# Windowed attention and two feed-forward nets on one core: the attention's loads in another order, and two pairs of small VectorE operations made one each

## The chip, the cores and the metric

The kernel runs on one core of a Trainium2 chip. The metric is the device time of one execution in microseconds (us), the median over repeated executions. Lower is better.

## What is computed

The reference, cut to what matters:

```python
# batch 4, 8 heads, 512 local and 32 global positions, head size 64, all float32
k_all, v_all = concat([k_g, k_l]), concat([v_g, v_l])
out_g = sm(scale * q_g @ k_all.T) @ v_all                 # global rows see everything
s_ll  = where(abs(i - j) <= 32, scale * q_l @ k_l.T, -1e9)   # local rows see a window
out_l = sm(concat([scale * q_l @ k_g.T, s_ll])) @ v_all   # ... and all global rows
# sm(s): e = exp(s - max(s)); e / (sum(e) + 1e-9)
x = concat([out_g, out_l]) as 2176 rows of 512
h = x @ w_in;  x = (h * cos(h)) @ w_out                   # net 1, 512 -> 2048 -> 512
out = relu(x @ w2_in) ** 2 @ w2_out                       # net 2, same sizes
```

The weights of the nets come as 64-bit numbers, of which the kernel takes the float32 value by operations on their two halves.

## The kernel before

The attention is cut into 40 items. Per batch and per group of four heads there are four local items (a pair of heads, half of the 512 positions each) and then one global item (the 32 global rows of the four heads). A group of four heads is called g0, g1, ... g7 here. Each engine executes its instructions in the order in which they stand in the program, so the program's order is a hand-made pipeline: the loop at line 1365 runs over steps, and in step s each stage treats item s minus the stage's lag. `CFG['order']` says in which order the stages stand within a step, `CFG['lag']` gives the lags. The stages are TRK and KEV and KC (transpose keys on TensorE, copy them out on ScalarE, double them on GpSimd), TRQ and QE (queries), S (scores, TensorE), SM (maximum and exponential), RC (reciprocal of the sum), NM (normalization, GpSimd and one VectorE operation), TM (transposes of the probabilities), TE (their way out of PSUM, ScalarE), OM (product with the values), OE (result to `xt`, VectorE). `BG`, `CB` and `CC` hold background work of the first net that is spread over the steps: loading raw weights and converting them, splitting operands into two halves.

Loads are issued on SyncE's queue (SP), which also works in program order. For each group there are loads of keys (`kn`, LK, five transfers), queries (`qn`, LQ, four transfers), values (`va`, LV, six transfers) and a copy of the values in SBUF, shifted by 64 rows (`vb`, CV, two transfers). `va`, `vb`, `kn` and `qn` have two buffers, so g2 overwrites g0. The two values tiles are `va_93` and `va_94`, their shifted copies `vb_95` and `vb_96`. The global values, padded (`vgz`, four transfers), global queries (`qgn`), key tails (`ktn`) and the raw weights of the first net (`raw`, one transfer of 512 KB each, two buffers) go through the same queue. Transfers take turns on eight semaphores, so a transfer is issued only when the one eight places before it has landed.

The prologue (lines 618 to 639) loads g0 and g1 except for g1's values; these are loaded at the end of step 2 (line 1424) and copied at the end of step 5 (line 1426). From g2 on the stages LK, LQ, LV and CV have lags 0, 1, 8 and 11, counted from the first item of the group two before.

A raw tile is read by three engines: ScalarE (line 147) and GpSimd (line 142) take its two halves, VectorE (lines 151 and 156) goes on with what they made. These stand in the engines' order at fixed steps: the first raw tile's in step 8, the second's ScalarE operation in step 11.

In a global item the scores lie in two PSUM banks. VectorE takes a maximum of each (line 541), then the maximum of both (line 546) and its product with -1/8 (line 547); ScalarE forms the exponentials and two sums (line 551); VectorE adds the sums (line 565), adds 1e-9 (line 568) and takes the reciprocal (line 571). All of these are one element per partition.

After the attention's last items the nets begin. Their order of work is planned by a list scheduler in the kernel itself, which is not touched.

Of the kernel before, what the change touches and what calls it, by code (L numbers as in the profile page):

```python
# [16 lines left out]
ALU = mybir.AluOpType  # L17
# [6 lines left out]
TWOPI = 2.0 * math.pi  # L24


CFG = {'order': ['CV', 'LQ', 'S', 'TE', 'BG', 'LK', 'OM', 'TRK', 'KEV', 'CC', 'SM',
           'RC', 'NM', 'CB', 'LV', 'OE', 'TRQ', 'QE', 'KC', 'TM'],
 'lag': {'S': 0,
         'TRK': -3,  # L30
         'TRQ': -2,
# [7 lines left out]
         'TE': 3,  # L39
         'OM': 4,  # L40
         'OE': 4,
         'LK': 0,
         'LQ': 1,
         'LV': 8,
         'CV': 11},
 'ndv': 1,
# [6 lines left out]
def kernel(  # L53
# [14 lines left out]
    nc = tc.nc  # L68
# [151 lines left out]
    BT, BG, BS, BO = (0, 1), (2,), (3, 4, 5), (6, 7)  # L220
# [20 lines left out]
    def whole(dst, src, c0, queues):  # L241

        n = dst.shape[2]
        if n == 2:
            for h, queue in enumerate(queues):
                queue.dma_start(dst[:, c0:4, h], src[h].rearrange("(c p) d -> p c d", p=P))
        else:
            for c in range(c0, 4):
                r = P * (c - c0)
                queues[0].dma_start(dst[:, c], src[:, r : r + P].rearrange("h p d -> p h d"))  # L250
# [10 lines left out]
    def load_q(gi, h=0, n=4, queues=(nc.sync, nc.sync)):  # L261
        b, g = gi // 2, slice(4 * (gi % 2) + h, 4 * (gi % 2) + h + n)
        if gi not in qn:
            qn[gi] = fp.tile([P, 4, 4, D], F32, tag="qn", name="qn", bufs=2)
        whole(qn[gi][:, :, h : h + n], q_l[b, g], 0, queues)

    def load_v(gi):
        b, h0 = gi // 2, 4 * (gi % 2)
        va, g = VA[gi % 2], slice(h0, h0 + 4)
        nc.sync.dma_start(va[0:SG, 0], v_g[b, g].rearrange("h p d -> p h d"))  # L270
        for c in range(5):
            r0, r1 = (SG if c == 0 else 0), (SG if c == 4 else P)
            nc.sync.dma_start(
                va[r0:r1, c],
                v_l[b, g, P * c - SG + r0 : P * c - SG + r1].rearrange("h p d -> p h d"),
            )
# [29 lines left out]
    def k_evac(p):  # L306
# [4 lines left out]
        if p == 0:  # L311
# [6 lines left out]
            )  # L318
        if CFG["kb"] == "A":
            nc.scalar.activation(  # L320
                t[:, :, 128:KTB], tk[:, 0:SG].unsqueeze(1).to_broadcast([P, 8, SG]), AF.Copy
            )
        elif CFG["kb"] == "D":
            nc.vector.tensor_copy(
# [3 lines left out]
    def k_copy(p):  # L328
# [4 lines left out]
        nc.gpsimd.tensor_scalar(t[:, 0:7, 64:128], t[:, 1:8, 0:64], **one)  # L333
        if CFG["kb"] == "P":
            nc.gpsimd.tensor_scalar(
# [52 lines left out]
    class Local:  # L388
# [48 lines left out]
        def recip(self):  # L437
            st = self.st
            return [
                lambda: nc.vector.tensor_scalar(  # L440
                    st[:, 2, :], st[:, 1, :], 1e-9, None, op0=ALU.add
                ),
                lambda: nc.vector.reciprocal(st[:, 2, :], st[:, 2, :]),
            ]

        def norm(self):
# [7 lines left out]
            for u in range(4):  # L454
                (nc.vector if u < CFG["ndv"] else nc.gpsimd).tensor_scalar(
                    self.pt[:, u, 0:P],
# [14 lines left out]
        def t_evac(self):  # L471
            self.tws = lp.tile([P, 4, P], F32, tag="tws", name="tws", bufs=2)
            self.tgs = lp.tile([P, P], F32, tag="tgs", name="tgs", bufs=2)
            nc.scalar.activation(self.tws, self.tw, AF.Copy)
            if CFG["teg"][self.hb] == "D":
                nc.vector.tensor_copy(self.tgs, self.tg)
# [28 lines left out]
        def o_evac(self):  # L505
            c0 = self.b * SL + 256 * self.hb
            dst, src = xt[:, self.kk, c0 : c0 + 256], self.o.rearrange("p i q -> p (i q)")
            if CFG["oe"][self.hb] == "D":
                nc.vector.tensor_copy(dst, src)
# [4 lines left out]
    class Global:  # L514
# [19 lines left out]
        def softmax(self):  # L534
            self.pt = lp.tile([P, 544], F32, tag="ptg", name="ptg", bufs=1)
            self.st = lp.tile([P, 8], F32, tag="stg", name="stg", bufs=2)
            st = self.st
            n = (320, 224)

            def top(i):  # L540
                nc.vector.tensor_reduce(
                    st[:, i : i + 1], self.s[i][:, 0 : n[i]], op=ALU.max, axis=AX.X
                )

            def rest():
                nc.vector.tensor_tensor(st[:, 2:3], st[:, 0:1], st[:, 1:2], op=ALU.max)
                nc.vector.tensor_scalar(
                    st[:, 2:3], st[:, 2:3], -0.125, None, op0=ALU.mult
                )
                for i in range(2):  # L550
                    nc.scalar.activation(
                        self.pt[:, 320 * i : 320 * i + n[i]],
                        self.s[i][:, 0 : n[i]],
                        AF.Exp,
                        bias=st[:, 2:3],
                        scale=0.125,
                        accum_out=st[:, 4 + i : 5 + i],
                    )

            return [lambda: top(0), lambda: top(1), rest]  # L560

        def recip(self):
            st = self.st
            return [
                lambda: nc.vector.tensor_tensor(
                    st[:, 6:7], st[:, 4:5], st[:, 5:6], op=ALU.add
                ),
                lambda: nc.vector.tensor_scalar(
                    st[:, 6:7], st[:, 6:7], 1e-9, None, op0=ALU.add
                ),  # L570
                lambda: nc.vector.reciprocal(st[:, 6:7], st[:, 6:7]),
            ]
# [64 lines left out]
    copy_v(0)  # L637
    load_k(1, 2, 2)
    load_q(1, 2, 2)
    nc.vector.memset(qgbd, 0.0)  # L640
    nc.gpsimd.memset(masks[0], 0.0)
    for h in range(2):
        s = slice(64 * h, 64 * h + 64)
# [16 lines left out]
    def spin(n):  # L660

        t = ps.tile([P, 512], F32, tag=f"bank{BO[1]}", name="spin")[:, 0:P]
        for _ in range(n):
            nc.tensor.matmul(t, lhsT=idle, rhs=idle, start=True, stop=True)
# [377 lines left out]
    S = [Step(s) for s in range(NS)]  # L1042
# [128 lines left out]
    order = [(s, i) for s in range(NS) for i in range(7)]  # L1171
# [193 lines left out]
    for s in range(L["TRK"], NI + L["OE"]):  # L1365
        due = lambda k: due_tr.get(s - k)
        qe = []
        for c in CFG["order"]:
            if c in ("BG", "CB", "CC"):
                for fn in bg[c].get(s, []):  # L1370
                    fn()
            elif c in ("TRK", "TRQ", "KEV", "KC", "QE"):
                p = due(L[c])
                if p is None:
                    continue
                if c == "TRK":
                    if p == 0:
                        spin(6)
                    tr_k(p)
                    if p == 0:  # L1380
                        spin(2)
                elif c == "TRQ":
                    qe = tr_q(p)
                    if p == 0:
                        spin(2)
                elif c == "KEV":
                    k_evac(p)
                elif c == "KC":
                    k_copy(p)
                elif c == "QE":  # L1390
                    for op in qe:
                        op()
            elif c in ("LK", "LQ", "LV", "CV"):
                p = due(L[c])
                if p is not None and p % 2 == 0 and p // 2 + 2 < 2 * B:
                    dict(LK=load_k, LQ=load_q, LV=load_v, CV=copy_v)[c](p // 2 + 2)
            else:
                i = it(s - L[c])
                if not i:
                    continue  # L1400
                if c == "S":
                    i.s_mm()
                    if s == 0:
                        prep_ktail(0)
                        k_tail(0)
                        k_tail(1)
                    elif s % 10 == 6 and s < 30:
                        prep_ktail(s // 10 + 1)
                    elif s % 10 == 3:
                        prep_qg(s // 10)  # L1410
                elif c == "SM":
                    for op in i.softmax():
                        op()
                elif c == "RC":
                    for op in i.recip():
                        op()
                else:
                    dict(NM=i.norm, TM=i.t_mm, TE=i.t_evac, OM=i.o_mm, OE=i.o_evac)[c]()
        if s in (8, 18):
            load_ktn(s // 10 + 2)  # L1420
        if s in (7, 17, 27):
            load_qgn(s // 10 + 1)
        if s == 2:
            load_v(1)
        if s == 5:
            copy_v(1)
        if due(0) is not None and due(0) // NPAIR + 1 < B:
            if due(0) % NPAIR == 2:
                load_vg(due(0) // NPAIR + 1)
        if s == XBOPEN:  # L1430
            first.close()
            open_pool("xb")
        if s == NI - 1:
            early.close()
            open_pool("s")
        if s >= NI - 1:
            emit(1.55 * (s - NI + 2))
# [39 lines left out]
```

## Time and profile before

| | |
|---|---|
| time, median of 3 runs | 874.62 us (874.11 to 876.35) |
| the profiled execution's own time | 874.08 us |
| its span, first to last instruction | 872.3 us |
| granted TensorE clock, mean | 0.997 of 2.4 GHz |
| TensorE (PE) busy | 849.8 us, 97% |
| VectorE (DVE) busy | 655.6 us, 75% |
| ScalarE (ACT) busy | 530.7 us, 61% |
| GpSimd (POOL) busy | 582.1 us, 67% |
| SP's queue (q1) | 130,736 packets, 179.79 MB, 62.5% of 16 DMA engines |

The span is what the profiler saw of one execution; the execution's time is 1.8 us longer. An engine's busy time leaves out waiting, issuing and branches. A timeline row gives start, length, engine, line, operation, output and inputs and, in brackets, the idle time of the engine just before it with what ended it. A row of the chain gives a piece of the sequence of work that ended last.

### The profile page before, as it was taken

What the parts mean: (1) busy time and instruction counts of PE and PEld (TensorE: products, weight loads), DVE (VectorE), ACT (ScalarE), POOL (GpSimd) and SP (SyncE); (2) the same over time, 40 slices, a digit from 0 to 9 for tenths busy, and PEclk for the clock granted to TensorE, in tenths of its full rate; (3) what the DMA queues carried; (4) which work ended last, traced back from release to release, by engine and by line L of the source; (5) the groups of instructions that cost most, each with busy time, mean ns of one, the idle gap of its engine ahead of it and who ended that gap; (6) DMA issues with size and microseconds to landing.
All of it is one profiled execution on the core that took longest, in us unless ns stands there. A gap on an engine that the chain in (4) does not pass through costs nothing.

```text
span 872.3 us, 17134 instructions
## 1 busy us (share of the span) xinstructions
PE 849.8 (97%) x6028; PEld 782.7 (90%) x6028; DVE 655.6 (75%) x1409; ACT 530.7 (61%) x1275; POOL 582.1 (67%) x666
## 2 busy tenths in 40 slices
PE   7899999999999999999999999999999999999998
PEld 5677777899999999999999998889888989899886
DVE  6589997999798777967788798996755767454544
ACT  5689787887776656666555867655544554342331
POOL 6479898899887564758258899976645647432221
PEclk9999999999999999999999999999999999999999
DMA  7898665447875576557727546566864686446633
GB/s 159 192 222 191 138 215 173 186 179 248 298 275 183 201 302 260 177 173 301 272 79 260 216 171 266 190 228 238 279 209 139 238 302 218 134 166 249 215 118 85
DMA packets 134261, 182.00 MB, mean 209 GB/s; under 512 B 60960, under 2 KB 114720, under 8 KB 134176
## 3 DMA queue, kind: packets, MB, share of 16 engines
q1 hardware_dynamic: 130736, 179.79, 62.5%
q10 hardware_dynamic: 3440, 1.11, 0.5%
q8 instruction: 48, 0.79, 0.4%
q14 instruction: 37, 0.30, 0.1%
HBM read 141.03 MB, written 35.65 MB: 203 GB/s over the span
## 4 chain that ended last, share of the span: by engine, by line
PE 84%; DVE 6%; POOL 5%; ACT 2%; DMA 2%; issue 1%; SPq 1%; POOLq 0%; DVEq 0%; ACTq 0%
PE y L943 40%; PE hb L851 16%; PE ha L851 10%; PE he L851 10%; PE s L400 2%; DMA vb<-va 1%; PE o L484 1%; POOL xs L172 1%; PE o L496 1%; DVE pt L416 1%; POOL g L172 1%; PE og L602 1%; PE tk L295 1%; PE tw L468 1%; POOL wf L163 1%
## 5 line engine op out<-in xcount | busy, mean ns | idle before, releaser
L172 POOL TENSOR_TENSOR g<-cr,g 128x384 fp32r<-128x384 f32 (+1 forms) x192 | 203.1, 1071 | 146.0 <-ACT g L902 140.1
L954 DVE TENSOR_TENSOR xt<-y,xt 128x384 f32<-128x384 f32 (+2 forms) x287 | 170.2, 595 | 95.4 <-PE y L943 93.3
L943 PE MATMUL y<-g,wo 128*128 128x384 f32 (+1 forms) x1152 | 219.2, 327 | 0.4 <-DVE xt L954 0.4
L943 PE MATMUL y<-wo,g 128*128 128x512 f32 x816 | 209.4, 393 | 0.0
L943 PEld LDWEIGHTS y<-g,wo 128*128 128x128 f32 x1152 | 194.1, 188 | 1.5 <-ACT wo L205 0.7
L943 PEld LDWEIGHTS y<-wo,g 128*128 128x128 f32 x816 | 150.0, 188 | 24.1
L851 PE MATMUL hb<-xs,wi 128*128 128x384 f32 (+1 forms) x864 | 166.3, 327 | 1.3 <-ACT cr L891 1.2
L851 PEld LDWEIGHTS hb<-xs,wi 128*128 128x128 f32 x864 | 146.8, 188 | 7.5 <-ACT cr L891 1.6
L851 PE MATMUL he<-xs,wi 128*128 128x384 f32 (+1 forms) x576 | 111.0, 327 | 1.6 <-DVE he L865 0.8
L851 PE MATMUL ha<-xs,wi 128*128 128x384 f32 (+1 forms) x576 | 110.9, 327 | 1.2 <-DVE cr L894 0.7
L902 ACT ACTIVATE g<-cr 128x384 fp32r<-128x384 f32 (+1 forms) x192 | 93.7, 501 | 20.4 <-DVE cr L894 19.3
L163 POOL TENSOR_TENSOR wf<-wf,cc 128x512 uint32<-128x512 uint32 x64 | 87.7, 1376 | 26.4 <-DVE wf L151 18.2
L851 PEld LDWEIGHTS he<-xs,wi 128*128 128x128 f32 x576 | 98.0, 188 | 6.2 <-DVE cr L894 1.5
L851 PEld LDWEIGHTS ha<-xs,wi 128*128 128x128 f32 x576 | 97.6, 188 | 4.0 <-DVE cr L894 1.0
L156 DVE SCALAR_TENSOR_TENSOR cc<-raw,cc 128x512 uint32<-128x512 uint32 x64 | 63.0, 990 | 0.0
L888 ACT ACTIVATE cr<-cr,halfpi 128x384 f32<-128x384 f32 (+1 forms) x96 | 55.9, 592 | 11.2 <-DVE cr L883 9.9
L426 ACT ACTIVATE pt<-pt,st 128x160 f32<-128x160 f32 x128 | 53.1, 423 | 2.4 <-DVE st L416 2.3
L151 DVE TENSOR_SCALAR wf<-wf 128x512 uint32<-128x512 uint32 x64 | 49.6, 779 | 4.3 <-POOL wf L142 3.1
L859 ACT ACTIVATE s<-hb 128x384 f32<-128x384 f32 (+1 forms) x48 | 22.7, 473 | 48.8 <-PE hb L851 48.7
L147 ACT ACTIVATE cc<-raw 128x512 uint32<-128x512 uint32 x64 | 42.4, 669 | 15.1 <-DMA raw<-in_moe_w_in_dram 9.6
L859 ACT ACTIVATE s<-he 128x384 f32<-128x384 f32 (+1 forms) x48 | 22.6, 471 | 32.9 <-PE he L851 32.7
L416 DVE CUSTOM_DVE_ANT_0 pt<-s,mask 128x160 f32<-128x160 f32 x128 | 33.7, 318 | 11.5 <-PE s L400 11.0
(147 smaller groups left out, 1331.8 us busy)
## 6 DMA issues: line engine op xcount, KB each, us to landing
xs<-xs_T SPq DMA_DIRECT2D x48, 768.0 KB, 5.7
xs<-xs_B SPq DMA_DIRECT2D x36, 768.0 KB, 5.3
raw<-in_moe_w_in_dram SPq DMA_DIRECT2D x32, 512.0 KB, 5.1
raw<-in_moe_w_out_dram SPq DMA_DIRECT2D x32, 512.0 KB, 4.7
xs<-xs_T SPq DMA_DIRECT2D x24, 640.0 KB, 5.7
xs_T<-xs SPq DMA_DIRECT2D x16, 768.0 KB, 4.2
xs<-xs_B SPq DMA_DIRECT2D x18, 640.0 KB, 5.6
xs_B<-xs SPq DMA_DIRECT2D x12, 768.0 KB, 5.0
```

The costliest lines, as they stand in the source:

```text
L151: V.tensor_scalar(u, u, 3, None, op0=ALU.logical_shift_left)
L156: V.scalar_tensor_tensor(v, t[:, :, 1].bitcast(U32), 0x80000000, v, op0=ALU.bitwise_and, op1=ALU.bitwise_or,)
L163: G.tensor_tensor(u, u, v, op=ALU.add)
L172: eng.tensor_tensor(lo, x, hi.bitcast(F32), op=ALU.subtract)
L416: nc.vector.tensor_tensor_reduce(out=self.pt[:, u, :], in0=self.s[u // 2][:, 160 * (u % 2) : 160 * (u % 2) + 160], in1=m, scale=-0.125, sc ...
L426: nc.scalar.activation(self.pt[:, u, :], self.pt[:, u, :], AF.Exp, bias=self.st[:, 0, u : u + 1], scale=-1.0, accum_out=self.st[:, 1, u : ...
L851: nc.tensor.matmul(out, lhsT=w[:, ws, c : c + P], rhs=xs[:, xh, kk, 0:n], start=start and k == 0, stop=k == 5, skip_group_check=True,)
L859: A.activation(self.sb[name], self.hold(bank_name), AF.Copy)
L888: A.activation(self.r[key], self.r[key], AF.Sin, bias=halfpi, scale=TWOPI)
L902: A.activation(GT[s, f][0][:, th * n : th * n + n], self.r[key], AF.Copy)
L943: nc.tensor.matmul(o, lhsT=l, rhs=r, start=k == 0, stop=k == 5)
L954: V.tensor_tensor(dst, y, dst, op=ALU.add)
```

## The change

The loads stand in another order. Within a step LK comes right after CV, then the scores and the product with the values, then LV, LQ and only then the background stage BG. The lags of LK and LQ grow from 0 and 1 to 2 and 3, so that keys and queries of g2 to g7 are loaded two steps later. The values of g1 are loaded in the prologue, and copied at the end of step 2 instead of step 5. In the global item the maximum and the factor become one operation with two steps, and so do the two sums and 1e-9.

```diff
-CFG = {'order': ['CV', 'LQ', 'S', 'TE', 'BG', 'LK', 'OM', 'TRK', 'KEV', 'CC', 'SM',
-           'RC', 'NM', 'CB', 'LV', 'OE', 'TRQ', 'QE', 'KC', 'TM'],
+CFG = {'order': ['CV', 'LK', 'S', 'TE', 'OM', 'LV', 'LQ', 'BG', 'TRK', 'KEV', 'CC', 'SM',
+           'RC', 'NM', 'CB', 'OE', 'TRQ', 'QE', 'KC', 'TM'],
...
-         'LK': 0,
-         'LQ': 1,
+         'LK': 2,
+         'LQ': 3,
          'LV': 8,
          'CV': 11},
...
             def rest():
-                nc.vector.tensor_tensor(st[:, 2:3], st[:, 0:1], st[:, 1:2], op=ALU.max)
                 nc.vector.tensor_scalar(
-                    st[:, 2:3], st[:, 2:3], -0.125, None, op0=ALU.mult
+                    st[:, 2:3], st[:, 0:1], st[:, 1:2], -0.125, op0=ALU.max, op1=ALU.mult
                 )
...
             return [
-                lambda: nc.vector.tensor_tensor(
-                    st[:, 6:7], st[:, 4:5], st[:, 5:6], op=ALU.add
-                ),
                 lambda: nc.vector.tensor_scalar(
-                    st[:, 6:7], st[:, 6:7], 1e-9, None, op0=ALU.add
+                    st[:, 6:7], st[:, 4:5], st[:, 5:6], 1e-9, op0=ALU.add, op1=ALU.add
                 ),
                 lambda: nc.vector.reciprocal(st[:, 6:7], st[:, 6:7]),
             ]
...
     load_q(1, 2, 2)
+    load_v(1)
     nc.vector.memset(qgbd, 0.0)
...
         if s == 2:
-            load_v(1)
-        if s == 5:
             copy_v(1)
```

TensorE, ScalarE and GpSimd have the same instructions in the same order as before. SP has the same transfers in another order, VectorE 16 instructions fewer.

On SP's queue, from the last load of the prologue before the change to the first raw tile (`va_94` and `vb_96` are g1's values and their copy, `kn` and `qn` with four heads are g2's keys and queries), before:

```order
L257 DMA kn<-in_k_g_dram 32x4x64
L258 DMA kn<-in_k_l_dram 96x4x64
L250 DMA kn<-in_k_l_dram 128x4x64 x3
L250 DMA qn<-in_q_l_dram 128x4x64 x4
L270 DMA va_94<-in_v_g_dram 32x4x64
L273 DMA va_94<-in_v_l_dram 96x4x64
L273 DMA va_94<-in_v_l_dram 128x4x64 x3
L273 DMA va_94<-in_v_l_dram 32x4x64
L117 DMA raw<-in_moe_w_in_dram 128x4x256
```

And with the change:

```order
L270 DMA va_94<-in_v_g_dram 32x4x64
L273 DMA va_94<-in_v_l_dram 96x4x64
L273 DMA va_94<-in_v_l_dram 128x4x64 x3
L273 DMA va_94<-in_v_l_dram 32x4x64
L257 DMA kn<-in_k_g_dram 32x4x64
L258 DMA kn<-in_k_l_dram 96x4x64
L250 DMA kn<-in_k_l_dram 128x4x64 x3
L280 DMA vb_96<-va_94 64x1024
L281 DMA vb_96<-va_94 64x1024
L250 DMA qn<-in_q_l_dram 128x4x64 x4
L117 DMA raw<-in_moe_w_in_dram 128x4x256
```

The values of g1 moved ahead of g2's keys, and their copy, which stood behind the first raw tile and g3's keys, now stands ahead of g2's queries and of that raw tile.

Further on the same queue, from there to the second raw tile (`kn` and `qn` are g3's now, `va_93` takes the values of g2), before:

```order
L257 DMA kn<-in_k_g_dram 32x4x64
L258 DMA kn<-in_k_l_dram 96x4x64
L250 DMA kn<-in_k_l_dram 128x4x64 x3
L280 DMA vb_96<-va_94 64x1024
L281 DMA vb_96<-va_94 64x1024
L286 DMA vgz_98<-in_v_g_dram 32x4x64 x4
L250 DMA qn<-in_q_l_dram 128x4x64 x4
L379 DMA qgn<-in_q_g_dram 32x8x64
L117 DMA raw<-in_moe_w_in_dram 128x4x256
L270 DMA va_93<-in_v_g_dram 32x4x64
```

And with the change:

```order
L286 DMA vgz_98<-in_v_g_dram 32x4x64 x4
L257 DMA kn<-in_k_g_dram 32x4x64
L258 DMA kn<-in_k_l_dram 96x4x64
L250 DMA kn<-in_k_l_dram 128x4x64 x3
L379 DMA qgn<-in_q_g_dram 32x8x64
L270 DMA va_93<-in_v_g_dram 32x4x64
L273 DMA va_93<-in_v_l_dram 96x4x64
L273 DMA va_93<-in_v_l_dram 128x4x64 x3
L273 DMA va_93<-in_v_l_dram 32x4x64
L250 DMA qn<-in_q_l_dram 128x4x64 x4
L117 DMA raw<-in_moe_w_in_dram 128x4x256
```

All transfers that stood ahead of the second raw tile still do, and the six of g2's values as well.

On VectorE, in the first global item (`stg` holds its maxima, sums and reciprocal), before:

```order
L541 TENSOR_REDUCE stg<-sg 128x1 x2
L546 TENSOR_TENSOR stg<-stg 128x1
L547 TENSOR_SCALAR stg<-stg 128x1
L440 TENSOR_SCALAR st<-st 128x4
L443 RECIPROCAL st<-st 128x4
```

And with the change (line 546 is now the fused operation; the same happens to lines 565 and 568):

```order
L541 TENSOR_REDUCE stg<-sg 128x1 x2
L546 TENSOR_SCALAR stg<-stg 128x1
L440 TENSOR_SCALAR st<-st 128x4
L443 RECIPROCAL st<-st 128x4
L455 TENSOR_SCALAR pt<-pt,st 128x128
```

One instruction is gone there and the others stand as they did.

## Rows read from the trace of the kernel before

**Rows 1.** Stretch: length; PE, PEld, DVE, ACT, POOL busy us; clock, DMA share, GB/s.

```profile
225.00:872.00 647.00, 641.29 (x3561) 604.04 (x3560) 467.39 (x788) 355.90 (x737) 394.67 (x369) 1.00 0.61 214
```

**Rows 2.** The chain of waits, its longest piece: start, us, what.

```profile
34.31 6.17 DMA vb<-va
```

**Rows 3.** TensorE's timeline, steps 8 to 10 and 14 to 15.

```profile
34.31 0.66 PE L350 MATMUL tq<-ident,qn 128*128 128x128 f32 x4
...
40.61 0.34 PE L496 MATMUL o<-tws,vb 128*64 128x64 f32 x4 [3.65 <-DMA vb<-va]
...
45.88 0.66 PE L350 MATMUL tq<-ident,qn 128*128 128x128 f32 x4
...
57.55 0.29 PE L496 MATMUL o<-tws,vb 128*64 128x64 f32 x4
...
61.82 0.66 PE L350 MATMUL tq<-ident,qn 128*128 128x128 f32 x4
```

**Rows 4.** Busy time by stretch again, columns as in rows 1: the stretch of that wait.

```profile
40.00:45.00 5.00, 4.39 (x45) 3.58 (x47) 0.63 (x2) 2.75 (x8) 1.28 (x4) 0.66 0.91 230
```

**Rows 5.** SP's timeline: start, us of issuing, transfers of one kind.

```profile
20.71 0.44 SPq L257 DMA_DIRECT2D kn<-in_k_g_dram  x1
...
23.36 2.10 SPq L250 DMA_DIRECT2D qn<-in_q_l_dram  x4
...
30.05 0.52 SPq L117 DMA_DIRECT2D raw<-in_moe_w_in_dram  x1
...
33.27 1.00 SPq L280 DMA_DIRECT2D vb<-va  x1
34.31 1.40 SPq L281 DMA_DIRECT2D vb<-va  x1
...
41.47 0.44 SPq L117 DMA_DIRECT2D raw<-in_moe_w_in_dram  x1
...
45.68 0.42 SPq L379 DMA_DIRECT2D ktn<-in_k_l_dram  x1
```

**Rows 6.** Line 117, the second raw tile's transfer alone: issue to landing.

```profile
DMA to landing us min/median/max: 4.6/4.6/4.6
```

**Rows 7.** Line 273 for g2's values: ns to issue, first and last start; landing.

```profile
L273 SPq DMA_DIRECT2D va<-in_v_l_dram x5: 384/435/642, 42.5 to 45.0; - x5
...
DMA to landing us min/median/max: 3.8/4.0/4.3
```

**Rows 8.** ScalarE's timeline, steps 8 to 12.

```profile
34.61 0.69 ACT L147 ACTIVATE cc<-raw 128x512 uint32<-128x512 uint32 x1 [0.21 <-DMA raw<-in_moe_w_in_dram]
...
42.26 0.60 ACT L308 ACTIVATE kT<-tk 128x512 f32<-128x512 f32 x1 [4.67 <-PE tk L295]
...
47.72 0.71 ACT L147 ACTIVATE cc<-raw 128x512 uint32<-128x512 uint32 x1
...
51.91 0.60 ACT L308 ACTIVATE kT<-tk 128x512 f32<-128x512 f32 x1 [1.23 <-PE tk L295]
```

**Rows 9.** GpSimd's timeline, then VectorE's, at the first raw tile.

```profile
34.66 0.68 POOL L142 TENSOR_SCALAR wf<-raw 128x512 f32<-128x512 f32 x1 [0.55 <-PE tq L350]
...
35.37 0.61 DVE L151 TENSOR_SCALAR wf<-wf 128x512 uint32<-128x512 uint32 x1 [0.70 <-POOL wf L142]
```

**Rows 10.** VectorE's groups by line, first 160 us: busy us, mean ns | idle before.

```profile
L565 DVE TENSOR_TENSOR stg<-stg 128x1 f32<-128x1 f32 x8 | 3.0, 376 | 0.0
L546 DVE TENSOR_TENSOR stg<-stg 128x1 f32<-128x1 f32 x8 | 1.9, 240 | 0.3
...
L547 DVE TENSOR_SCALAR stg<-stg 128x1 f32<-128x1 f32 x8 | 1.2, 154 | 0.3
```

**Rows 11.** The chain of waits again: its pieces on lines 546 and 565 (first, longest, last).

```profile
61.94 0.11 DVE stg L565
...
96.00 0.90 DVE stg L565
...
129.15 0.55 DVE stg L565
```

## The prediction

> **What bounds the kernel now.** I read the busy time by stretch first. From 225 us on, the two nets keep TensorE busy for 641.29 of 647 us [rows 1]; the change touches nothing there, so what it can win lies in the attention, the first 155 us, and reaches the end as a shift of everything behind it. The chain of waits says where the attention loses most: one piece of 6.17 us in which it runs through a transfer, the second half of the copy of g1's values [rows 2]. TensorE's timeline shows the same from its side: it stands idle for 3.65 us before the first product with that copy [rows 3]. In the stretch from 40 to 45 us its granted clock is 0.66, so part of it ran at the lower level of 1.2 GHz instead of 2.4, after that idle time [rows 4]. That costs something more: from the first product with `vb` to the queries' transpose it takes 45.88 - 40.61 = 5.27 us, while the same sequence one group later takes 61.82 - 57.55 = 4.27 us [rows 3]. So 1.0 us goes to the clock, and **3.65 + 1.0 = 4.65 us** is all that this stall can give back.
>
> Next I read SP's queue, since the copy waited for its turn there. From 20.71 us (g2's keys) to 41.47 us (second raw tile) SP issues 32 transfers without a pause, 20.76 / 32 = 0.65 us each [rows 5]. The queue is full; what is moved forward pushes back all that it passes. So the question is what stands behind the copy and who needs it when. ScalarE's timeline answers: at 34.61 it starts on the first raw tile after waiting 0.21 us for its landing, thus that tile is late already; and it takes the second at 47.72, where that one, issued at 41.47, had landed 4.6 us later, at 46.1 [rows 5, 6, 8].
>
> **The copy and g1's values.** The values (6 transfers) now come right at 20.71 and g2's keys (5) next, so the copy is issued after 11 transfers, at 20.71 + 11 x 0.65 = 27.9 us; with the 6.17 us that it took before [rows 2] it lands by 34.0. TensorE asks for it at 40.61 - 3.65 = 36.96 [rows 3]. The stall goes, with 2.9 us to spare.
>
> **g2's keys and queries** are pushed back by 6 and 8 transfers. The last of the queries is issued some 16 x 0.65 = 10.4 us after 20.71, at 31.1, and lands at about 35.7 if it takes the 4.6 us of rows 6; TensorE transposes them at 34.31 [rows 3]. A wait of about 1 us, and one of like size for the keys one step earlier, can appear. I cost them at nothing, because the next item covers them.
>
> **The first raw tile** is passed by the copy. The copy's two issues took 1.00 and 1.40 us in the full queue [rows 5]; at the best pace seen, 2.10 us for four [rows 5], they take 1.05. The tile lands 1.05 to 2.4 us later than 34.6, at 35.7 to 37.0. Three engines hang on it: ScalarE (behind it on that engine stand the exponentials of step 8), GpSimd (behind it the normalization, for which TensorE's transposes wait) and VectorE, which already waits 0.70 us for GpSimd's part [rows 8, 9]. Between this operation and the next keys' way out of PSUM at 42.26 ScalarE has 42.26 - 34.61 - 4.67 = 2.98 us of work [rows 8]. So that point comes at 38.6 to 40.0, 3.6 to 2.3 us earlier than before. I take 2.3: the two issues were measured in just this place.
>
> **The second raw tile** is passed by the six transfers of g2's values; all that stood ahead of it still does. It changes places with them, so it lands where the last of them did: last issue 45.0, landing about 4.0 us later, 49.0 [rows 7]. By issues: between the end of its own issue at 41.9 and the next load at 45.68 lie 3.8 us [rows 5], so 41.47 + 3.8 + 4.6 = 49.9. The low end is the pace of 0.525 us for all 38 transfers ahead: 20.71 + 20.0 + 4.6 = 45.3. The high end is 0.65 us: 20.71 + 24.7 + 4.6 = 50.0. ScalarE wants the tile at 47.72 less what was won, and its engine is in order, so that operation now starts at 49.0, 1.3 us later than before. Behind it ScalarE was idle for 1.23 us before the keys at 51.91 [rows 8]; that takes up all but 0.05 us. I take **+0.05 us** for the whole of the loads, between 3.6 us won (first raw tile at its early end, second at 45.3: 47.72 + 1.23 - 45.3 = 3.65) and 1.05 us lost (50.0). In other words, the 4.65 us come back as two waits for raw weights.
>
> **The loads of g3 to g7** move within a queue that runs ahead of its readers: TensorE waits for no load in the attention after 40.61 in the trace. The copies of values gain on g4's and later keys (five transfers, 3.2 us), the keys have that much in hand, since they are still issued five steps ahead of their transpose. Costed at nothing; the cover is those steps.
>
> **VectorE.** Sixteen instructions go: eight of line 546 (mean 240 ns) and eight of line 565 (376 ns); each fused one is costed as line 547 (154 ns), with two steps on one element [rows 10]. That is 1.9 + 3.0 = 4.9 us of VectorE, but most is beside the path: the chain runs through these two lines in five pieces, the first, longest and last of which are 0.11, 0.90 and 0.55 us, together 2.1 us [rows 11]. Bounds: 0 (TensorE is held elsewhere at the same time) and 2.1. The plain operation costs 0.15; the rest of the long ones is waiting, and the operation behind may meet it too. I take 5 x 0.19 (the operation and a step to the next) = **0.95 us won**.
>
> On that waiting a page of the Trainium skill has a rule: "SBUF — State Buffer", section "Who interferes with whom", says that a VectorE operation with two inputs in SBUF can be shut out by a GpSimd operation that reads SBUF, and one with a single input outside the two-port modes can not. The trace agrees as far as it goes: the two-input lines have means of 240 and 376 ns, the one-input line 154 [rows 10]. By the rule alone the waits would go with the operations and the full 2.1 us would be won, 1.15 us more than I take.
>
> **The sum** against the profiled execution, 874.08: + 0.05 - 0.95 = 873.2. The median of the three runs stands 0.54 us above that execution, so I expect a median of **873.7 us**. A measurement of this kernel can tell 0.3%, 2.6 us, from no change.
>
> **Rivals.**
> - *The raw tiles come sooner* (0.20). SP issues at its best pace since the transfers are better mixed. For it: 0.525 us was seen [rows 5]; against it: no stretch of 32 kept it. The first tile then bounds, 3.6 us are won, with VectorE 4.55: 870.1 us.
> - *The stall goes whole* (0.06). Neither tile holds anyone. Against it: the first one holds ScalarE, GpSimd and VectorE even now. 4.65 + 0.95: 869.0 us.
> - *Slower* (0.12). TensorE is now idle twice, in step 9 for the first tile and in step 12 for the second, and its clock falls after each, as it did after the one idle time before [rows 3, 4]; the second fall costs another 1.0 us. If the tile lands at 51.0, 2.05 us are lost on top. 874.62 + 2.05 + 1.0 - 0.95 = 876.7 us. It decides from a landing later than 47.72 + 1.23 = 48.95 us.
> - *The change doesn't do what it says* (0.04): the copy still lands after 36.96, because the values ahead of it are late by over 2.9 us. Then little is different from before but VectorE's part: 873.7 us, within my forecast.
>
> **Chances.** The forecast itself has 0.58. Its own range runs from 872.5 (the full 2.1 us on VectorE) to 875.7 (a tile at 50.0, nothing on VectorE). Range: 870.1 to 876.7, from the first rival to the third; the whole stall and the worse half of the slow case stay out, about 0.15. Faster by over 2.6 us: the second rival whole, the first in most cases, a little of the forecast, 0.25. Slower by over 2.6 us: half of the slow rival and a little for a load that I costed at nothing, 0.10. Within: 0.65.
>
> **What would show it.** In the new profile TensorE has no wait for `vb` near 37 us. ScalarE's line 147 waits for its load twice, starting near 37 and near 49, and GpSimd's line 142 near 37. The keys' way out of PSUM near 51.9 (step 12) stands where it stood. Lines 547 and 568 of before have no counterpart beyond the fused ones, which take about 154 ns, never 900. I am wrong if the second raw tile lands before 47 us, if TensorE is past step 12 more than 2 us earlier or later, or if a load that I costed at nothing stops TensorE after 55 us.

## The result, and the profile after

The changed kernel takes **879.5 us** (median of 7 runs, 878.92 to 883.74) against 874.11 us of the kernel before in the same comparison (7 runs, 873.3 to 876.35): ratio 1.0065, 95% interval 1.0047 to 1.0084. It is slower by 5.4 us, and the predicted 873.7 us (870.1 to 876.7) was wrong. The profiled execution took 879.26 us, with a span of 877.5 against 872.3 us: 5.2 us more.

The nets are not the cause. The row that answers to [rows 1] shows TensorE busy for all but 5.6 us of the last 652; before, it was all but 5.7 of 647. The other rows are stretches in the attention. Columns as in rows 1.

```profile
225.00:877.00 652.00, 646.44 (x3591) 608.89 (x3589) 470.88 (x798) 359.34 (x744) 402.37 (x373) 1.00 0.61 214
35.00:40.00 5.00, 4.55 (x41) 3.31 (x42) 1.86 (x5) 2.62 (x10) 2.26 (x5) 0.66 0.64 145
...
50.00:55.00 5.00, 1.78 (x13) 1.43 (x17) 1.51 (x5) 4.63 (x19) 2.39 (x6) 0.71 1.11 222
55.00:60.00 5.00, 5.00 (x64) 4.22 (x58) 3.13 (x15) 2.83 (x13) 2.44 (x6) 0.50 0.14 30
60.00:65.00 5.00, 5.00 (x48) 3.69 (x47) 2.61 (x8) 1.35 (x4) 2.65 (x6) 0.77 0.96 203
```

Two stretches of low clock stand there where before had one [rows 4]. From 50 to 55 us TensorE hardly works; from 55 to 60 it has no idle time and gets half its clock. TensorE's timeline shows what came ahead of each, and answers to [rows 3]:

```profile
35.45 0.47 PE L350 MATMUL tq<-ident,qn 128*128 128x128 f32 x1 [1.28 <-DMA qn<-in_q_l_dram]
...
39.01 0.28 PE L496 MATMUL o<-tws,vb 128*64 128x64 f32 x4
...
43.27 0.66 PE L350 MATMUL tq<-ident,qn 128*128 128x128 f32 x4
...
53.22 1.11 PE L468 MATMUL tw<-ident,pt 128*128 128x128 f32 x4 [3.95 <-ACT tws L587]
...
63.06 0.28 PE L496 MATMUL o<-tws,vb 128*64 128x64 f32 x4
```

And the transposes of step 12 in the kernel before:

```profile
51.72 0.60 PE L468 MATMUL tw<-ident,pt 128*128 128x128 f32 x4
```

The wait for `vb` is gone. Put beside [rows 3], the same work stands as follows:

| TensorE's work | before | after | shift |
|---|---|---|---|
| first product with g1's `vb` (step 9) | 40.61 | 39.01 | -1.60 |
| queries' transpose one item later | 45.88 | 43.27 | -2.61 |
| transposes of step 12 | 51.72 | 53.22 | +1.50 |
| product with `vb` in step 14 | 57.55 | 63.06 | +5.51 |
| span | 872.3 | 877.5 | +5.2 |

So 2.61 us were won by 43 us; a new wait of 3.95 us turned that into a loss of 1.50; and between 53.22 and 63.06 us, with no wait, another **4.0 us** went while the clock was low: this work took 63.06 - 53.22 = 9.84 us, and 57.55 - 51.72 = 5.83 before. ScalarE's timeline (it answers to [rows 8]) tells what the wait was for:

```profile
37.38 0.68 ACT L147 ACTIVATE cc<-raw 128x512 uint32<-128x512 uint32 x1 [3.67 <-DMA raw<-in_moe_w_in_dram]
...
40.37 0.60 ACT L308 ACTIVATE kT<-tk 128x512 f32<-128x512 f32 x1
...
50.37 0.67 ACT L147 ACTIVATE cc<-raw 128x512 uint32<-128x512 uint32 x1 [4.79 <-DMA raw<-in_moe_w_in_dram]
...
52.58 0.58 ACT L587 ACTIVATE tws<-twg 128x512 f32<-128x512 f32 x1
...
53.22 0.57 ACT L308 ACTIVATE kT<-tk 128x512 f32<-128x512 f32 x1
```

ScalarE stood at the second raw tile for 4.79 us. Behind that operation in its order stand four exponentials and the way out of PSUM (`tws`, line 587), whose end released TensorE. SP's timeline and the landing of line 117's two transfers, the counterparts of [rows 5, 6]:

```profile
27.32 0.47 SPq L280 DMA_DIRECT2D vb<-va  x1
27.83 0.60 SPq L281 DMA_DIRECT2D vb<-va  x1
...
31.60 0.51 SPq L117 DMA_DIRECT2D raw<-in_moe_w_in_dram  x1
...
42.32 2.27 SPq L250 DMA_DIRECT2D qn<-in_q_l_dram  x4
44.64 0.51 SPq L117 DMA_DIRECT2D raw<-in_moe_w_in_dram  x1
```

```profile
DMA to landing us min/median/max: 5.7/5.7/5.8
```

The second raw tile is issued at 44.64 instead of 41.47 us, and lands at 44.64 + 5.7 = 50.3 instead of 46.1. The chain of waits runs through just these transfers where it ran through the copy before [rows 2]:

```profile
31.04 4.36 DMA qn<-in_q_l_dram
...
44.64 5.71 DMA raw<-in_moe_w_in_dram
```

The theory from here on, **A**: the place of the second raw tile, behind ten transfers of its step (six of values, four of queries), makes the second wait, and the clock that falls after it makes the larger part of the loss. The rivals, **B**: the first wait (g2's queries) or the fused operations cause it.

### The profile page after: what moved, and what is told of

It reads as the page before. It is cut to its first block, busy times and chain, and to the rows that moved or that the text cites. A ratio compares the mean times of both kernels' runs of the same rounds, so it can differ in the third digit from the quotient of the medians.

```text
span 877.5 us, 17106 instructions
## 1 busy us (share of the span) xinstructions
PE 854.8 (97%) x6028; PEld 786.5 (90%) x6028; DVE 650.2 (74%) x1393; ACT 531.4 (61%) x1275; POOL 585.6 (67%) x666
## 4 chain that ended last, share of the span: by engine, by line
PE 82%; POOL 7%; DMA 3%; DVE 2%; ACT 2%; issue 1%; SPq 1%; POOLq 0%; ACTq 0%; DVEq 0%
PE y L940 40%; PE hb L848 16%; PE ha L848 10%; PE he L848 10%; DMA raw<-in_moe_w_in_dram 2%; PE s L400 1%; POOL g L172 1%; POOL wf L163 1%; POOL xs L172 1%; POOL pt L455 1%; PE tw L468 1%; DMA vb<-va 1%; PE o L484 1%; PE og L598 1%; PE o L496 1%
## 5 line engine op out<-in xcount | busy, mean ns | idle before, releaser
L172 POOL TENSOR_TENSOR wi<-ws,wi 128x512 fp32r<-128x512 f32 x23 | 31.3, 1364 | 16.6 <-ACT wi L196 12.2
```

The costliest lines, as they stand in the source:

```text
L172: eng.tensor_tensor(lo, x, hi.bitcast(F32), op=ALU.subtract)
```

## The experiments

Each batch had runs of the kernel before on its own chip; differences to it in microseconds are those of the medians in one batch (874.57 us in that of the raw tiles first, the values alone, the fusions alone and the second wait; 875.3 in that of the table, the loads alone and the two by need; 874.5 in that of both waits and the second tile alone).

**Raw tiles first.** The loads of raw weights become a stage of their own behind LK and ahead of the values and queries; all engines but SP keep their order.

```diff
-CFG = {'order': ['CV', 'LK', 'S', 'TE', 'OM', 'LV', 'LQ', 'BG', 'TRK', 'KEV', 'CC', 'SM',
+CFG = {'order': ['CV', 'LK', 'RL', 'S', 'TE', 'OM', 'LV', 'LQ', 'BG', 'TRK', 'KEV', 'CC', 'SM',
...
-        bg["BG"].setdefault(s, []).append(lambda: conv_load(*k))
+        bg["RL"].setdefault(s, []).append(lambda: conv_load(*k))
```

> The changed kernel, but a raw tile's load stands ahead of the values' and queries' loads of its step (other engines unchanged). Theory A, the second raw tile behind ten transfers (six of g2's values, four of g3's queries) makes the second wait and its low clock: the tile lands near 43 instead of 50.35 us, TensorE has no wait at step 12, the 2.5 us won by step 10 stay, so about 871.7 us. Theory B, the loss comes from the first wait (step 8) or from the fused operations: the second wait may go, but the time stays at 878 to 880 us.

Measured: 871.42 us (870.3 to 872.78), ratio to the kernel before 0.9962 (0.995 to 0.9973). ScalarE's line 147 and the stretches:

```profile
37.34 0.66 ACT L147 ACTIVATE cc<-raw 128x512 uint32<-128x512 uint32 x1 [3.00 <-DMA raw<-in_moe_w_in_dram]
45.24 0.72 ACT L147 ACTIVATE cc<-raw 128x512 uint32<-128x512 uint32 x1
```

```profile
50.00:55.00 5.00, 5.00 (x89) 4.01 (x83) 4.68 (x20) 4.30 (x20) 4.36 (x11) 1.00 1.00 222
55.00:60.00 5.00, 4.76 (x72) 3.93 (x68) 3.69 (x18) 3.88 (x12) 3.96 (x9) 1.00 0.83 185
```

The second tile is taken without a wait, the clock stays whole, and the shift won by step 10 is kept. The first tile is as late as in the changed kernel (taken at 37.34 us), and it does stop TensorE: VectorE waits 3.45 us for GpSimd's part of that tile, its copy of the transposed queries (line 356) stands behind, and TensorE waits for that copy before it transposes the next keys:

```profile
39.47 0.66 PE L295 MATMUL tk<-ident,kn 128*128 128x128 f32 x4 [1.99 <-DVE qT L356]
```

In the changed kernel, where TensorE had first waited for g2's queries and then run at a low clock, the same transposes start at 39.67 us. So that first wait and its low clock cost some 0.2 us at most; the first raw tile would have held TensorE until then anyway. A holds.

**The second tile alone.** The same, for one transfer only.

```diff
-        bg["RL"].setdefault(s, []).append(lambda: conv_load(*k))
+        bg["RL" if i == 1 else "BG"].setdefault(s, []).append(lambda: conv_load(*k))
```

> The changed kernel with one instruction moved: the load of the second raw tile is issued ahead of its step's values and queries, the other raw tiles stay behind them. Theory A (the place of this one transfer is the whole loss): 871 to 872.5 us, ratio 0.995 to 0.998, the second raw tile landed at 43 to 45 us, no second wait. Rival B (the third and fourth tiles, which the run with all raw tiles first moved too, have a part in what that run won): 873 to 876 us.

Measured: 872.66 us (871.87 to 873.14), ratio 0.9978 (0.9964 to 0.9992), 0.16 us above A's band and below B's. It is 1.8 us under the kernel before, where the changed kernel is 5.4 us above it: moving this one instruction is worth 7.2 us, against 8.5 with all raw tiles moved (874.57 - 871.42 = 3.15 under the kernel before). The intervals of the two runs overlap, so whether the later tiles have a part in the difference stays open. Their profiles show none: TensorE waits for no later raw tile in either, and in both it waits for the transposed queries (1.99 us with all tiles first), but here a lower clock follows, and the next queries' transpose starts at 44.34 us instead of 43.09.

```profile
39.45 0.66 PE L295 MATMUL tk<-ident,kn 128*128 128x128 f32 x4 [2.11 <-DVE qT L356]
```

```profile
40.00:45.00 5.00, 4.96 (x52) 3.98 (x52) 4.14 (x19) 4.81 (x18) 3.75 (x8) 0.66 1.03 220
```

**Matmuls in the second wait.** The changed kernel, with 16 matmuls on the idle tile ahead of the wait of step 12; nobody reads their product.

```diff
+                    if s == 12:
+                        fill(16)
```

> The changed kernel with 16 products of a tile of zeros put into TensorE's wait at step 12 (some 3.5 of 3.95 us), whose results nobody reads. Theory A, second half: of the 5.4 us lost, 4.0 us are the low clock after that wait: 875 to 876 us, and the clock in the stretch from 55 to 60 us is 1.00 instead of 0.50. If the clock is not the cost: 879.5 us or more.

Measured: 876.62 us (875.32 to 880.65), ratio 1.0028 (1.0017 to 1.0039): 2.1 us above the kernel before and so 3.3 us better than the changed kernel, 0.6 us above A's band, though the wait's cause is untouched. The profiled execution was one of the longer ones (878.36 us): its first wait was 1.68 us, and the second raw tile landed at 53.25 us. TensorE's timeline (each of the 16 matmuls stands twice in the trace) and two stretches:

```profile
51.85 3.74 PE L668 MATMUL spin<-idle 128*128 128x128 f32 x32
56.12 0.66 PE L468 MATMUL tw<-ident,pt 128*128 128x128 f32 x4 [0.54 <-ACT tws L587]
```

```profile
50.00:55.00 5.00, 5.00 (x69) 4.71 (x62) 1.60 (x10) 1.73 (x7) 2.13 (x5) 1.00 1.06 237
55.00:60.00 5.00, 4.46 (x75) 3.68 (x74) 3.41 (x17) 4.94 (x22) 2.74 (x7) 1.00 0.45 76
```

The work behind the wait, which had taken 9.84 us, now runs at full clock and takes 62.01 - 56.12 = 5.89 us, and of the 4.0 us most is back in the median. So they are the clock's, and no data behind the wait is late.

**Matmuls in both waits.** In addition 7 ahead of the query transposes of step 8.

```diff
+                    if s == 8:
+                        fill(7)
                     qe = tr_q(p)
```

> The changed kernel with matmuls on the idle tile in both of TensorE's waits: 7 of them ahead of the query transposes of step 8 (the wait of 1.3 us at 34 us) and 16 ahead of the wait of step 12 (3.9 us). They add to no result. Theory A (both waits stay as long as they are, but each is followed by a stretch at half clock that costs by itself: some 1.5 us after the first, 4.0 after the second): clock 1.00 from 35 to 65 us, 873.5 to 875.5 us, ratio 0.999 to 1.001. Rival B (the time lost after a wait is not the clock's, the clock only shows it, or the filling matmuls hold TensorE as long as they spare): 876.5 us or more, like the run that filled the second wait alone.

Measured: 876.24 us (875.73 to 882.79), ratio 1.0036 (1.0013 to 1.006): 1.7 us above the kernel before and between both bands, so filling the first wait as well won nothing that can be told. The profiled execution was the longest of the six. In it TensorE arrived earlier, the same 16 matmuls ended earlier, and 2.77 us of the wait stayed open:

```profile
49.79 3.74 PE L668 MATMUL spin<-idle 128*128 128x128 f32 x32
56.30 0.65 PE L468 MATMUL tw<-ident,pt 128*128 128x128 f32 x4 [2.77 <-ACT tws L587]
```

```profile
55.00:60.00 5.00, 3.71 (x44) 2.89 (x45) 2.49 (x10) 4.15 (x17) 2.73 (x7) 0.69 0.61 105
60.00:65.00 5.00, 5.00 (x39) 3.89 (x41) 2.84 (x12) 2.52 (x10) 3.12 (x5) 0.50 0.51 117
```

Only this one execution has a profile; the mean granted clock of all six goes the same way: the four executions with a mean granted clock of 0.997 to 0.999 took 875.73 to 876.45 us, the two with 0.993 and 0.995 took 882.79 and 879.48.

**g1's values alone.** The kernel before, with only the prologue's part of the change.

```diff
+    load_v(1)
...
         if s == 2:
-            load_v(1)
-        if s == 5:
             copy_v(1)
```

> The kernel before, with g1's values loaded in the prologue and copied at the end of step 2, nothing else. Theory A: the stall before the first product with the copy goes, nothing new passes the second raw tile, which lands at 46 us as before; the first raw tile is held up by the two transfers of the copy: 871 to 873 us. Theory B, whoever removes the stall meets the first raw tile instead and pays with the clock: 874 to 878 us.

Measured: 874.32 us (872.04 to 876.35), ratio 0.9996 (0.9986 to 1.0006). A's 871 to 873 was missed. The time lies in B's 874 to 878, and as B said TensorE meets the first raw tile: it waits 1.42 us for the copy of the transposed queries, which stands behind that tile on VectorE. But it does not pay with the clock. TensorE was 2.9 us ahead in step 10 (queries' transpose at 43.00 us instead of 45.88), and gave it back in pieces (ScalarE's timeline, then TensorE's):

```profile
47.97 0.69 ACT L147 ACTIVATE cc<-raw 128x512 uint32<-128x512 uint32 x1 [2.67 <-DMA raw<-in_moe_w_in_dram]
```

```profile
50.84 0.66 PE L468 MATMUL tw<-ident,pt 128*128 128x128 f32 x4 [1.84 <-ACT tws L591]
57.70 0.34 PE L496 MATMUL o<-tws,vb 128*64 128x64 f32 x4 [0.81 <-DMA vb<-va]
```

Here too the second raw tile is the next thing late (47.95 us, taken at 47.72 before [rows 8]), and then g2's copy. The clock stayed at 1.00 from 35 to 65 us. This is the case that the prediction drew for the whole change, a gain that comes back as waits and nothing more.

**The table of orders and lags alone.**

```diff
-CFG = {'order': ['CV', 'LQ', 'S', 'TE', 'BG', 'LK', 'OM', 'TRK', 'KEV', 'CC', 'SM',
-           'RC', 'NM', 'CB', 'LV', 'OE', 'TRQ', 'QE', 'KC', 'TM'],
+CFG = {'order': ['CV', 'LK', 'S', 'TE', 'OM', 'LV', 'LQ', 'BG', 'TRK', 'KEV', 'CC', 'SM',
+           'RC', 'NM', 'CB', 'OE', 'TRQ', 'QE', 'KC', 'TM'],
...
-         'LK': 0,
-         'LQ': 1,
+         'LK': 2,
+         'LQ': 3,
```

> The kernel before with the change's table of stage orders and lags alone; the values of step 1's second group are loaded and copied where they were, nothing is fused. Theory A (the place of the raw tiles behind the values and queries of their step makes the second wait, whoever issues vb): second raw tile landed at 49 to 51 us, ScalarE and TensorE wait for it, and 877 to 880 us, ratio 1.003 to 1.007. Rival B (the two moves only hurt together, since the group's values are then still issued at 27 to 34 us and TensorE reaches the raw tile's step later): the first stall stays, the raw tile is in time for a late TensorE, 873.5 to 875 us, ratio 0.999 to 1.001.

Measured: 882.83 us (881.77 to 883.55), ratio 1.0088 (1.0072 to 1.0104): 7.5 us above the kernel before, worse than both expected. ScalarE's and TensorE's rows:

```profile
51.64 0.67 ACT L147 ACTIVATE cc<-raw 128x512 uint32<-128x512 uint32 x1 [7.83 <-DMA raw<-in_moe_w_in_dram]
```

```profile
54.48 1.12 PE L468 MATMUL tw<-ident,pt 128*128 128x128 f32 x4 [6.96 <-ACT tws L591]
```

B was wrong that the first stall would stay: with g2's keys and queries moved back, the wait for g1's copy shrinks from 3.65 to 0.91 us even from the copy's old place. TensorE runs 4.4 us ahead (queries' transpose at 41.52 us instead of 45.88), meets the late raw tile sooner, idles longer, and from 55 to 65 us has a clock of 0.50. A has the place right and its size too small.

**The loads alone.** The changed kernel with the fusions undone.

```diff
+                nc.vector.tensor_tensor(st[:, 2:3], st[:, 0:1], st[:, 1:2], op=ALU.max)
...
+                lambda: nc.vector.tensor_tensor(
+                    st[:, 6:7], st[:, 4:5], st[:, 5:6], op=ALU.add
+                ),
```

> The changed kernel with the two VectorE fusions undone, so only the loads are moved. Theory A (the whole loss comes from the loads: the second raw tile lands some 50 us behind ten transfers, TensorE idles a second time and its clock falls): about 879.5 to 880.2 us, ratio to before 1.006 to 1.007, second raw tile landed at 50 or later, granted clock under 0.8 in two of the three slices from 50 to 65 us. Rival B (the fused instructions have a part in the loss, by their place beside GpSimd): 876 to 878 us, as the loads alone would then lose less than the change.

Measured: 881.33 us (879.44 to 884.12), ratio 1.0072 (1.0053 to 1.0091). That is 6.0 us above the kernel before and 1.1 us above A's band. The loads lose all of it; the fusions have no part in the loss. The profile separates the two waits as well: the one near 39 us (1.43 us, for VectorE's copy of the queries) left the clock at 1.00 up to 50 us, and the one of step 12 (4.37 us) was followed by 0.80, 0.50 and 0.68 in the three stretches from 50 to 65 us. So the loss comes without a low clock behind the first wait, and with that B falls.

**The fusions alone**, in the kernel before (the reverse of that diff).

> The kernel before with the two fused VectorE operations alone. By the prediction's term: 0.95 us won, 873.2 us (within 872.0 to 874.1). By the rule that the waiting goes with the second input: up to 2.1 us won, 872.0 us. If the fused operations made the loss: 879 us.

Measured: 873.84 us (872.76 to 875.44), ratio 0.9996 (0.9987 to 1.0004). That is in the expected range of 872.0 to 874.1, and by the interval at most 1.1 us are won.

**By need.** Raw tiles first, and the copy of g1's values back behind the first raw tile.

```diff
-        if s == 2:
+        if s == 5:
             copy_v(1)
```

> The kernel with the raw tiles in a stage of their own ahead of values and queries (as in the run that put them first), and the conversion of the group's values back behind the first raw tile's on ScalarE and GpSimd. Theory A: neither wait is left, the second raw tile lands at 43 to 45 us, clock 1.00 from 35 to 65 us, 869.5 to 871.5 us, ratio 0.994 to 0.997. Rival B (the conversion now comes too late for TensorE's first use of the group's values, so a wait of 1 to 3 us at some 38 us is back): 872 to 875 us.

Measured: **870.43 us** (869.69 to 871.9), ratio 0.9949 (0.9934 to 0.9964): the best kernel here, 4.9 us under the one before, and in A's band. Of B's account the wait near 38 us is there, but short and without its price; the clock is 1.00 from 35 to 65 us all the same:

```profile
37.98 0.34 PE L496 MATMUL o<-tws,vb 128*64 128x64 f32 x4 [1.08 <-DMA vb<-va]
```

**By need, without the fusions.** The same kernel with the two pairs apart again, as in the diff of the loads alone.

> The same with the two fusions undone. This prices the fusions where no load stalls the first 65 us. Theory A (the fused instructions save VectorE 1.9 us in all, of which at most half lies on the path): 0.2 to 1.0 us slower than the fused kernel of this batch. Rival B (a VectorE instruction with two SBUF operands is held up beside GpSimd, so taking half of them out is worth the full saving): 1.5 to 2.1 us slower.

Measured: 871.8 us (870.37 to 873.1), ratio 0.9962 (0.9949 to 0.9976): 1.4 us above the fused one, between the two bands, and the intervals overlap. Three pairs now price the fusions: 874.57 - 873.84 = 0.7 us in the kernel before, 6.0 - 5.4 = 0.6 with the loads moved, 1.4 here. None is more than its intervals leave uncertain; all point the same way. The third is not the fusions' price alone: in its profile TensorE met no wait for a load after 25 us and stood ahead of the fused kernel (the scores of step 15 at 54.78 us instead of 57.23), and lost that only near the attention's end, in a wait of 1.44 us for an exponential at 138.90 us and a clock of 0.91 in the 20 us from 125 and again from 145. A gain at 60 us does not always reach the end.

## Why the prediction was wrong, by its own steps

**The copy and g1's values: right.** Predicted issue 27.9 us, landing by 34.0; issued at 27.32 and 27.83, the second half landed at 32.35, and TensorE has no wait for `vb`. What could be won was bounded rightly too: 2.61 us by step 10, and the best kernel wins 4.9 us in all, 3.5 without the fusions.

**First raw tile: right, a little late.** Predicted landing 35.7 to 37.0, measured 37.4. The keys' way out of PSUM gained 42.26 - 40.37 = 1.9 us, 2.3 predicted. g2's queries did stop TensorE, for 1.28 us as expected, and the tile covered that (39.67 against 39.47 us with the raw tiles first).

**Second raw tile: mechanism right, landing mis-sized.** "Last issue 45.0, landing about 4.0 us later, 49.0": the issue came at 44.64, but the transfer took 5.7 us. I had taken the landing of smaller loads in [rows 7] for a tile of 512 KB, and 4.6 us from a single row [rows 6] as the other way. By the prediction's own working, a landing at 50.35 costs 50.35 - 48.95 = 1.40 us; the transposes of step 12 came 1.50 us late.

**The step that failed: "I take +0.05 us for the whole of the loads".** A gain of 2.3 us that ends in ScalarE's wait means that TensorE, 2.3 us ahead, stands idle in step 12 as well. The prediction says so itself ("the 4.65 us come back as two waits"), yet charges the wait for its length alone and leaves the clock after it to the slow rival, there at 1.0 us because the one row at hand showed 1.0. It cost 4.0. With the measured terms, 874.08 + 1.50 + 4.01 less 0.3 (from 5.51 in step 14 to 5.2 in the span) gives 879.3; the execution took 879.26. These are shifts read from that very execution, so the sum tests nothing; it shows that no other loss is left over. Its own sign of being wrong came with it: TensorE was past step 12 2.12 us late (the next scores at 54.47 us instead of 52.35), and the sign was set at 2.

The 1.0 us was too low by its own row as well. The sequence that served as measure holds an idle 0.24 us, so the low clock of the kernel before cost some 1.2 us:

```profile
60.07 0.77 PE L400 MATMUL s<-kT,qT 64*64 64x160 f32 x14 [0.24 <-ACT ptg L551]
```

**The slow rival was the case, with one price wrong.** The idle time in step 12 and the point of decision (a landing later than 48.95) are what the trace shows; the first idle time was in step 8, for g2's queries, and not in step 9 for the raw tile (there it was with the raw tiles first, the second tile alone and the loads alone). Its 876.7 us is too low because of the clock's 4.0 us.

**VectorE: the waits went, the time hardly.** Each row gives the count and then the shortest, median and longest duration in ns of a line's eight instructions, before:

```profile
L546 DVE TENSOR_TENSOR stg<-stg x8: 159/160/730, 19.6 to 141.4; 128x1 f32<-128x1 f32 x8
...
L565 DVE TENSOR_TENSOR stg<-stg x8: 144/276/968, 25.3 to 144.9; 128x1 f32<-128x1 f32 x8
```

and after:

```profile
L546 DVE TENSOR_SCALAR stg<-stg x8: 214/214/216, 19.5 to 146.3; 128x1 f32<-128x1 f32 x8
...
L564 DVE TENSOR_SCALAR stg<-stg x8: 201/210/214, 24.6 to 149.9; 128x1 f32<-128x1 f32 x8
```

The long ones, 730 and 968 ns, are gone. Both had ended together with an operation of GpSimd: at 58.82 us (GpSimd's at 58.81) and at 96.89 us (96.87). That agrees with the rule of the Trainium skill ("SBUF — State Buffer", section "Who interferes with whom"), by which a VectorE operation with a single input in SBUF, outside the two-port modes, is not shut out by GpSimd, if the scalar operand of the fused ones isn't counted as an input and they run outside those modes, which no run here shows by itself. But the fused ones take 201 to 216 ns, not the 154 that I costed. The three pairs of runs say 0.6, 0.7 and 1.4 us, about my 0.95; the 2.1 us that the rule alone would give were reached in none of them, and the first pair's interval, at most 1.1 us, excludes them in the kernel before.

## What to carry to other kernels

A stall that is taken away on a full queue moves to the next transfer that its engines need in order; before pricing the change, list what each engine waits for next and ask how far ahead of it the faster engine will arrive. Where the new wait leaves TensorE idle, price the stretch of low clock behind it as a term of the sum, with a range up to the longest such stretch seen in any trace, not as a footnote. And when three engines need one transfer soon, issue it ahead of the loads of its step that are needed later: here moving that one instruction was worth 7.2 us.

## What the hardware showed that was not expected

The low clock (0.50, the level of 1.2 GHz) lasted very unequally long. After 3.65 us of idle time, the kernel before had it for some 3.4 us; here are its stretches of 1 us:

```profile
41.00:42.00 1.00, 1.00 (x16) 0.93 (x12) 0.42 (x1) 0.00 (x0) 0.00 (x0) 0.81 0.74 160
42.00:43.00 1.00, 1.00 (x7) 0.88 (x5) 0.00 (x0) 0.74 (x2) 0.06 (x1) 0.50 0.83 190
...
44.00:45.00 1.00, 1.00 (x16) 0.56 (x10) 0.21 (x1) 1.00 (x3) 0.08 (x1) 0.50 1.11 330
45.00:46.00 1.00, 1.00 (x25) 0.93 (x22) 0.97 (x10) 0.96 (x6) 0.00 (x0) 0.98 1.12 202
```

After 3.95 us the changed kernel had it for some 10 us, with TensorE busy all the while from 53.22 on:

```profile
52.00:53.00 1.00, 0.00 (x0) 0.00 (x0) 0.25 (x2) 1.00 (x5) 0.00 (x0) 0.55 1.10 233
53.00:54.00 1.00, 0.79 (x4) 0.79 (x5) 0.96 (x4) 1.00 (x4) 0.73 (x2) 0.50 1.33 197
...
61.00:62.00 1.00, 1.00 (x5) 0.53 (x6) 0.00 (x0) 0.77 (x2) 0.70 (x1) 0.50 0.96 218
62.00:63.00 1.00, 1.00 (x12) 0.60 (x10) 0.49 (x2) 0.00 (x0) 0.00 (x0) 0.83 0.82 185
```

Nor did a wait of like length always bring it: 1.99 us with the raw tiles first left 1.00 from 35 to 65 us and 1.43 us with the loads alone 1.00 from 35 to 50, 2.11 us with the second tile alone was followed by 0.66, and 1.28 us in the changed kernel by 0.66 as well. What decides this the runs don't tell, and it stays open.
